# Chunked attention and a snake MLP on one core: first V load in two parts, second-layer matmuls dealt out later, one square moved from GpSimd to ScalarE

## Chip, cores and metric

The kernel runs on one NeuronCore of a Trainium2 chip. The metric is the device time of one execution in microseconds (us), given as the median of several runs. Engines are TensorE (PE: matmuls; PEld: its weight loads), VectorE (DVE), ScalarE (ACT), GpSimd (POOL) and SyncE (SP).

## The reference, cut to what matters

There are 4 batches, 8 heads, 768 positions and a head size of 64. Each chunk of 32 queries attends to 8 memory keys and to a window of keys from 16 before the chunk to 8 after it. The result, 3072 tokens of 512, goes through an MLP of width 2048.

```python
for c in range(S // 32):
    l_start, r_end = max(0, 32 * c - 16), min(S, 32 * c + 32 + 8)
    k_full = concat([mem_k, k[:, :, l_start:r_end]]); v_full = concat([mem_v, v[:, :, l_start:r_end]])
    out[:, :, 32 * c:32 * c + 32] = softmax(q_c @ k_full.T / 8) @ v_full
x = out.transpose(0, 2, 1, 3).reshape(3072, 512)
h = x @ w_in
g = h + sin(alpha * h) ** 2 / (alpha + 1e-9)
result = g @ w_out
```

## The kernel before

The batches are worked through one after the other, and each engine runs its instructions in the order in which the program issues them.

**Attention.** The queries of a head are cut into 8 blocks of 96 (`QW`, `NJ`). For one cell (a pair of heads and a block) the scores are one matmul per head, whose 128 rows are the keys of that block with the memory keys among them (`qk`, L265 to L275). A unit is four cells. `exps` (L277) takes the exponentials on ScalarE, three to four instructions a unit, masked by the bias. `pv` (L294) multiplies them with V, 65 columns a head, of which the last gives the sum, and VectorE divides (L305, L306). `xt` (L313) transposes the block on TensorE and copies it to `xT` (L325). V stands in `vws`, one buffer for even and one for odd batches; `load_v` (L126) fills heads times blocks `n0` to `n1` with four DMAs on GpSimd's queue (L139): two large ones and two for the rows that neighbouring blocks share.

**The first burst.** `first_burst` (L348) does batch 0's attention in an order written out by hand in `ORDER` (L14): `k`, `q` turn a pair of heads of K and Q by transposes, `s` are a unit's scores, `e` its exponentials, `v` its product with V, `x` its transposes and copy, and `z` warming matmuls on zeros (`spin`, L157; each 128x512). `xt` adds two of these ahead of its transposes for the units whose block has a PSUM tile of its own (units 2 to 7, L316). After `e 7` a sine of one column is taken, which brings in ScalarE's table for sines (L375). The copies of units 4, 5 and 6 are ScalarE's, the others VectorE's.

**Loads at the start.** GpSimd's queue issues, in this order: K and Q of batch 0 in pairs of heads with V's first 16 (heads 0 and 1) among them, V 16 to 32, V 32 to 64 (heads 4 to 7), four quarters of w_in (`load_w_in`, L201), K and Q of batch 1 (`load_qk`, L117), two halves of w_out (`load_w_out`, L207).

**The first MLP layer.** `l1` does one of 16 groups (ft) of 128 features for the 768 tokens of a batch: eight matmuls of 384 columns into one PSUM tile `hT` of two banks (L400), or for ft 3, 7 and 11 of batch 0 into two tiles `hs` of the small pool (`split`); a sine on ScalarE (L412, or L409 in halves); and a square, which a string of letters gives to DVE, ACT or POOL (L518 to L520; L421, L415, L417). `finish` then combines on VectorE: `gT = s / alpha + hT` (L429, or L425 in halves). `finish` of a group is called in the loop's next step, ahead of that step's `l1`. In batch 0 the one of ft 11 is held back (`late`, L529) until that of ft 12 is issued. The pool `big` (PSUM) has three buffers of two banks for scores, products and `hT`, the pool `smp` two of one bank for the second layer's `o`, for transposes and for `hs`.

**The second MLP layer.** `l2` (L440) is a generator of 96 matmuls a batch, 16 for each of 6 blocks of 128 tokens, 128x512 each (L449, L479; for batch 0 the first two blocks go in halves, so that they end at matmuls 24 and 32). A finished block is copied (`put_out`, L437; even blocks VectorE, odd ones ScalarE) and stored by SyncE. The class `Stream` (L24) deals these matmuls out: `take(n)` adds n to a debt and issues matmuls until it is paid; without `through`, it also returns at the end of a block and keeps the rest of the debt for the next call.

**The order of the main loop** (L499). For each batch: 16 steps of the first layer, with `take(2)` in each from ft 1 on (`take(3)` in the last batch) of the batch before; then this batch's second layer joins the stream; then, in batch 0 alone, K and Q of batch 1 are turned in eight pieces with 4 + 8 x 3 matmuls between; in batches 1 and 2 those of the next batch were turned within the 16 steps. Then `burst` (L330) does the next batch's attention in steps of one block, with the step's entry of `shares` dealt in three parts between scores, product and transposes (the product lags by 3 steps in the first such burst and by 1 in the others), and then `take(3)`. The last batch's 96 matmuls run alone at the end.

Of the kernel before, what the change touches and what calls it, by code (L numbers as in the profile page):

```python
# [12 lines left out]
KW = 856  # L13
ORDER = (  # L14
    "k 0,q 0,memk 0,memv 0,k 1,s 0,e 0,z 1,s 1,e 1,q 1,k 2,s 2,e 2,s 3,v 0,q 2,e 3,k 3,x 0,v 1,q 3,s 4,e 4,x 1,"
    "s 5,e 5,z 1,v 2,s 6,e 6,z 2,v 3,x 2,v 4,s 7,e 7,x 3,v 5,x 4,v 6,x 5,v 7,x 6,x 7"
)
BF = mybir.dt.bfloat16
F32 = mybir.dt.float32
ACTF = mybir.ActivationFunctionType  # L20
# [29 lines left out]
def kernel(  # L50
# [12 lines left out]
    nc = tc.nc  # L63
# [25 lines left out]
    rows = consts.tile([P, 6], F32, name="rows")  # L89
# [36 lines left out]
    def load_v(b, n0, n1):  # L126


        vw = vws[b % 2].rearrange("p h j c -> p (h j) c")
        vf = v[b].rearrange("h s d -> (h s) d")  # L130
        vf = vf.rearrange("(n p) d -> p n d", p=QW)
        parts = (
            (vw[16:64, n0:n1, 0:D], vf[0:48, n0:n1]),
            (vw[72:120, n0:n1, 0:D], vf[48:96, n0:n1]),
            (vw[0:16, n0 + 1:n1, 0:D], vf[80:96, n0:n1 - 1]),
            (vw[120:128, n0:n1 - 1, 0:D], vf[0:8, n0 + 1:n1]),
        )
        for dst, src in parts:
            nc.gpsimd.dma_start(dst, src)  # L139
# [14 lines left out]
    zeros = consts.tile([P, 512], BF, name="zeros")  # L154
    nc.vector.memset(zeros[:], 0.0)  # L155

    def spin(n, z=None):  # L157

        if z is None:
            z = smp.tile([P, 512], F32, name="z", tag="sm")  # L160
        for _ in range(n):
            nc.tensor.matmul(z[:], zeros[:, 0:P], zeros[:])  # L162
# [26 lines left out]
        out=biasm[:], in0=rows[:, 0:5], scalar1=1.0, scalar2=-NEG, op0=ALU.subtract, op1=ALU.mult)  # L189
    nc.scalar.copy(memk_bf[:], memk_f[:])  # L190
    load_v(0, 16, 32)
    load_v(0, 32, 64)
    with nc.allow_non_contiguous_dma(reason="alpha transpose load"):
        nc.sync.dma_start(alpha_sb[:], moe_alpha.rearrange("(ft p) -> p ft", p=P))

# [81 lines left out]
    def exps(cells, sc):  # L277
        pt = pts[state["n"] % NPT]
        state["n"] += 1
        for m in range(3):  # L280
            cols = [((1 if j == 0 else 0), 4, (2 if j == NJ - 1 else 3))[m] for _, j in cells]
            c0 = 0
            for c1 in range(1, 5):
                if c1 < 4 and cols[c1] == cols[c0]:
                    continue
                nc.scalar.activation(  # L286
                    pt[:, 0:H * QW].rearrange("p (g e c) -> p e g c", g=4, e=2)[:, :, c0:c1, 32 * m:32 * m + 32],
                    sc[:, :, 0:4 * QW].rearrange("p g (e c) -> p g e c", e=4)[:, :, c0:c1, 32 * m:32 * m + 32],
                    ACTF.Exp, bias=biasm[:, cols[c0]:cols[c0] + 1], scale=0.125,
                )  # L290
                c0 = c1
        return pt
# [17 lines left out]
        )  # L310
        return x_blk, ot

    def xt(dst, x_blk, ot, copy=nc.vector.tensor_copy):  # L313
        if ot is None:
            z = smp.tile([P, 512], F32, name="z", tag="sm")
            spin(2, z)  # L316
            xtp = z[:].bitcast(BF)[:, 0:KT * QW]
        else:
            xtp = ot[:].bitcast(BF)[:, 0, 640:640 + KT * QW]
        xtp = xtp.rearrange("p (k c) -> p k c", k=KT)  # L320
        for kt in range(KT):
            nc.tensor.transpose(  # L322
                xtp[:, kt, :], x_blk[:, 2 * kt:2 * kt + 2, :].rearrange("p e d -> p (e d)"), ident[0:QW, 0:QW]
            )
        copy(dst, xtp)  # L325
# [4 lines left out]
    def burst(b, stream, shares, lag):  # L330

        xT = xp.tile([P, KT, S], BF, name="xT")
        ptl, xbl = {}, {}
        for s in range(NJ + lag + 1):
            n = shares[s] if s < len(shares) else 0
            if s < NJ:
                ptl[s] = exps(row(s), qk(row(s)))
            stream.take(n // 3, True)
            if 0 <= s - lag < NJ:
                xbl[s - lag] = pv(b, row(s - lag), ptl.pop(s - lag))  # L340
            stream.take((n + 1) // 3, True)
            if 0 <= s - lag - 1 < NJ:
                j = s - lag - 1
                xt(xT[:, :, QW * j:QW * j + QW], *xbl.pop(j))
            stream.take((n + 2) // 3, True)
        return xT

    def first_burst(kq):  # L348

        xT = xp.tile([P, KT, S], BF, name="xT")  # L350
        cells = [[(u // 2, 4 * (u % 2) + c) for c in range(4)] for u in range(8)]
        scl, ptl, xbl = {}, {}, {}
        for what, n in [t.split() for t in ORDER.split(",")]:
            n = int(n)
            if what == "k":
                t_k(kq[0], n)
            elif what == "q":
                t_q(kq[1], n, nc.vector.tensor_copy if n == 1 else nc.scalar.copy)
            elif what == "memk":
                mt = smp.tile([P, HP, 32], BF, name="mt", tag="sm")  # L360
                for hp in range(HP):
                    nc.tensor.transpose(
                        mt[:, hp, :],
                        memk_bf[0:32, 2 * hp:2 * hp + 2, :].rearrange("p e d -> p (e d)"),
                        ident[0:32, 0:32])
                nc.vector.tensor_copy(memkT[:], mt[:])
                put_memk(0)
            elif what == "memv":
                put_memv(0)
            elif what == "s":  # L370
                scl[n] = qk(cells[n])
            elif what == "e":
                ptl[n] = exps(cells[n], scl.pop(n))
                if n == 7:
                    nc.scalar.activation(rows[:, 0:1], zeros[:, 0:1], ACTF.Sin)  # L375
            elif what == "z":
                spin(n)
            elif what == "v":
                x_blk, ot = pv(0, cells[n], ptl.pop(n))
                xbl[n] = x_blk, (ot if n < 2 else None)  # L380
            elif what == "x":
                hf = n % 2
                xt(xT[:, n // 2, HALF * hf:HALF * hf + HALF].rearrange("p (k c) -> p k c", k=KT),
                   *xbl.pop(n), nc.scalar.copy if n in (4, 5, 6) else nc.vector.tensor_copy)
        return xT


# [106 lines left out]
    stream = Stream()  # L494
    xT = first_burst(kq)
# [3 lines left out]
    for i in range(B):  # L499
        gT = gp.tile([P, FT, S], BF, name="gT")  # L500
        last = i == B - 1
        at_ft = {2 * n: n for n in range(8)}
        pieces = []
        if not last:
            srcs = [(kq_next[n % 2], n // 2) for n in range(2 * HP)]
        state["pools"] = 1

        def pair_to(n):
            while len(pieces) < min(n, 2 * HP):
                pieces.append(pair_up(*srcs[len(pieces)], nc.vector.tensor_copy if i == 0 and len(pieces) in (2, 4, 6) else None))  # L510

        def piece(n):
            pair_to(n + 3)
            (t_k if n % 2 == 0 else t_q)(pieces[n], n // 2)

        if 0 < i < B - 1:
            pair_to(2)
        finish, late = None, None  # L518
        for ft in range(FT):
            sq = ("DADPADAPADAPDAAA" if i == 0 else "ADAAPDADADAPADAD")[ft]  # L520
            if 1 <= ft:
                stream.take(3 if last else 2)
            if 0 < i < B - 1 and ft in at_ft:
                piece(at_ft[ft])
            if i == 0 and ft == 8:
                pair_to(2)
            if i == 0 and ft == 13:
                load_v(1, 0, H * NJ)
            if finish is not None and ft - 1 == 11 and i == 0:  # L529
                late = finish  # L530
            elif finish is not None:
                finish()
                if late is not None:
                    late()
                    late = None
            finish = l1(i, ft, xT, gT, sq, i == 0 and ft in (3, 7, 11))
        finish()
        stream.add(l2(i, gT, last))
        if not last:
            if i == 0:  # L540
                state["pools"] = 0
                stream.take(4)
                for n in range(2 * HP):
                    piece(n)
                    stream.take(3, True)
                put_memv(1)
            if i + 2 < B:
                kq_next = load_qk(i + 2)
            if i == 0:
                xT = burst(i + 1, stream, (5, 5, 5, 4, 4, 4, 4, 4, 3, 3, 3, 3), 3)  # L550
            else:
                xT = burst(i + 1, stream, (16, 8, 6, 6, 6, 5, 5, 5, 5, 5), 1)
            if i + 2 < B:
                put_memk(i + 2)
            stream.take(3)
            if i + 2 < B:
                load_v(i + 2, 0, H * NJ)
                put_memv(i + 2)
# [31 lines left out]
```

The softmax here doesn't subtract the row's maximum and nothing guards it: scores larger than these inputs give would overflow.

## Time and profile before

| What | Value |
|---|---|
| median of 7 runs | 233.82 us (233.18 to 234.45) |
| profiled execution | 233.18 us |
| its span in the profile | 231.4 us |
| busy: PE, DVE, ACT, POOL | 219.4, 160.1, 152.3, 70.0 us |
| first layer's matmuls of batch 0 begin | 26.90 us |
| second layer's matmuls of the last batch end | 228.2 us |
| HBM read, written | 28.94 MB, 6.29 MB |

The span is the time between the first and last instruction of the profiled execution; all times of day in this document count from its start. A line of a view names the engine, the source line (L400 is line 400 of the kernel) and, as "out<-in", the tiles. Matmuls overlap, so one that is listed with 0.326 us (128x384) follows the one before it by less. An idle time in brackets is that of the engine just before the instruction, with what ended it.

### The profile page before, as it was taken

How to read it: one execution, taken by the hardware profiler on the slowest of the kernel's cores; microseconds unless marked ns; L12 is line 12 of the kernel's file. 1: busy time of each engine (PE TensorE's matmuls, PEld its weight loads, DVE VectorE, ACT ScalarE, POOL GpSimd, SP SyncE). 2: the span in 40 equal slices, each digit the busy share in tenths (PEclk: the TensorE clock that was granted, in tenths of full speed). 3: DMA queues.
4: the chain of work that ended last, by engine and by line, in shares of the span. 5: the costliest groups of instructions: out<-in, count | busy, mean ns of one | idle time of the engine just before them, and what ended most of it. 6: DMA issues, size and time to landing. Idle time of an engine off the chain costs nothing.

```text
span 231.4 us, 4595 instructions
## 1 busy us (share of the span) xinstructions
PE 219.4 (95%) x1842; PEld 122.7 (53%) x1842; DVE 160.1 (69%) x288; ACT 152.3 (66%) x246; POOL 70.0 (30%) x80
## 2 busy tenths in 40 slices
PE   7998899989999999999999999998999999899994
PEld 3455555555446556554555656664555555454453
DVE  5776588988568897987566789887565468784110
ACT  2578689793987387888664877978665676880110
POOL 8998122585812115167200314020000020100000
PEclk9999999999999999999999999999999999999999
DMA  6999999999999900119992101010111010101112
GB/s 85 151 174 177 204 204 206 208 145 88 175 223 158 92 30 0 48 8 191 164 151 73 45 0 48 0 45 3 45 48 70 24 47 0 45 0 48 73 64 91
DMA packets 51805, 21.13 MB, mean 91 GB/s; under 512 B 36296, under 2 KB 48840, under 8 KB 51784
## 3 DMA queue, kind: packets, MB, share of 16 engines
q0 software_dynamic: 45568, 14.41, 72.2%
q1 hardware_dynamic: 6216, 6.43, 9.3%
q8 instruction: 14, 0.23, 0.4%
q14 instruction: 7, 0.06, 0.1%
HBM read 28.94 MB, written 6.29 MB: 152 GB/s over the span
## 4 chain that ended last, share of the span: by engine, by line
PE 62%; ACT 12%; DVE 9%; POOL 7%; issue 5%; DMA 2%; POOLq 1%; DVEq 0%; ACTq 0%
PE o L479 28%; PE hT L400 21%; DVE gT L429 5%; ACT u L412 4%; POOL vw L139 3%; PE ot L301 3%; ACT pt L286 3%; PE sc L270 2%; DMA vw<-in_v_dram 2%; DVE s L421 2%; ACT s L415 2%; PE tt_a L242 2%; PE ot L322 2%; PE o L468 2%; PE o L449 1%
## 5 line engine op out<-in xcount | busy, mean ns | idle before, releaser
L479 PE MATMUL o<-w_out_sb,gT 128*128 128x512 bf16 x336 | 90.0, 380 | 0.4 <-DVE gT L429 0.4
L400 PE MATMUL hT<-xT,w_in_sb 128*128 128x384 bf16 x488 | 87.1, 326 | 2.9 <-DVE gT L429 2.8
L429 DVE SCALAR_TENSOR_TENSOR gT<-s,inv_alpha,hT 128x768 bf16<-128x768 f32 x61 | 61.0, 1012 | 19.7 <-ACT s L415 11.2
L412 ACT ACTIVATE u<-hT,alpha_sb 128x768 f32<-128x768 f32 x61 | 54.7, 897 | 24.5 <-PE hT L400 23.5
L400 PEld LDWEIGHTS <-w_in_sb 128*128 128x128 bf16 x512 | 49.3, 98 | 37.5 <-issue 3.8
L286 ACT ACTIVATE pt<-sc,biasm 128x256 bf16<-128x256 f32 (+2 forms) x104 | 39.1, 470 | 15.2 <-PE sc L270 15.2
L479 PEld LDWEIGHTS <-gT 128*128 128x128 bf16 x336 | 29.3, 98 | 24.3 <-DVE gT L429 1.2
L417 POOL TENSOR_TENSOR s<-u 128x768 f32<-128x768 f32 x9 | 13.2, 1465 | 87.5 <-ACT u L412 61.3
L415 ACT ACTIVATE s<-u 128x768 f32<-128x768 f32 x32 | 27.0, 843 | 1.0
L421 DVE TENSOR_TENSOR s<-u 128x768 f32<-128x768 f32 x23 | 24.3, 1056 | 2.3 <-ACT u L412 2.2
L306 DVE TENSOR_TENSOR x_blk<-ot,rinv 96x512 bf16<-96x512 f32 x32 | 22.0, 686 | 1.1
L139 POOL DMA_DIRECT2D vw<-in_v_dram x24 | 21.9, 925 | 0.2 <-issue 0.2
L216 POOL COPY pr<-q_bf 128x768 bf16<-128x768 bf16 x12 | 10.7, 895 | 35.5 <-PE tt_a L242 24.4
L437 DVE COPY o_sb<-o 128x512 f32<-128x512 f32 x12 | 8.3, 690 | 15.6 <-PE o L479 15.4
L437 ACT COPY o_sb<-o 128x512 f32<-128x512 f32 x11 | 6.4, 583 | 17.9 <-PE o L479 17.9
L305 DVE RECIPROCAL rinv<-ot 96x8 f32<-96x8 f32 x32 | 6.4, 201 | 15.7 <-PE ot L301 15.5
L301 PEld LDWEIGHTS <-pt 128*128 128x128 bf16 x256 | 11.7, 98 | 6.8 <-issue 2.5
L162 PE MATMUL z<-zeros 128*128 128x512 bf16 x40 | 12.8, 427 | 1.9 <-DVE zeros L155 1.2
L301 PE MATMUL ot<-vw,pt 128*128 128x65 bf16 x256 | 13.0, 193 | 1.0 <-DMA vw<-in_v_dram 0.4
L242 PEld LDWEIGHTS <-pr 128*128 128x128 bf16 x144 | 10.0, 98 | 5.9 <-DVE pr L216 0.9
L270 PEld LDWEIGHTS <-kTi 64*128 64x128 bf16 x256 | 6.8, 94 | 11.4 <-PE ot L322 5.5
L322 PEld LDWEIGHTS <-x_blk 96*128 96x128 bf16 x128 | 8.7, 97 | 7.3 <-DVE x_blk L306 1.5
(76 smaller groups left out, 170.0 us busy)
## 6 DMA issues: line engine op xcount, KB each, us to landing
out_dram<-o_sb SPq DMA_DIRECT2D x23, 256.0 KB, 2.5
k_bf<-in_k_dram POOLq DMA_DIRECT2D x3, 768.0 KB, 7.7
q_bf<-in_q_dram POOLq DMA_DIRECT2D x3, 768.0 KB, 12.6
vw<-in_v_dram POOLq DMA_DIRECT2D x6, 384.0 KB, 14.9
w_in_sb<-in_moe_w_in_dram POOLq DMA_DIRECT2D x4, 512.0 KB, 9.7
w_out_sb<-in_moe_w_out_dram POOLq DMA_DIRECT2D x2, 1024.0 KB, 24.2
k_bf<-in_k_dram POOLq DMA_DIRECT2D x4, 192.0 KB, 5.1
q_bf<-in_q_dram POOLq DMA_DIRECT2D x4, 192.0 KB, 5.2
```

The source lines that it names most:

```text
L139: nc.gpsimd.dma_start(dst, src)
L242: nc.tensor.transpose(t[:, r, :], src[:, r].rearrange("p e d -> p (e d)"), ident[:])
L286: nc.scalar.activation(pt[:, 0:H * QW].rearrange("p (g e c) -> p e g c", g=4, e=2)[:, :, c0:c1, 32 * m:32 * m + 32], sc[:, :, 0:4 * QW].re ...
L301: nc.tensor.matmul(otv[:, n // 4, n % 4, :], pt[:, QW * n:QW * n + P], vws[b % 2][:, 2 * hp + n % 2, j, 0:D + 1])
L306: nc.vector.tensor_tensor(out=x_blk[:].rearrange("p (g e) d -> p g e d", g=2), in0=otv[0:QW, :, :, 0:D], in1=rv.unsqueeze(3).to_broadcast( ...
L400: nc.tensor.matmul(hts[hf][:, 0:HALF], w_in_sb[:, kt, P * ft:P * ft + P], xT[:, kt, HALF * hf:HALF * hf + HALF], start=(kt == 0), stop=(kt ...
L412: nc.scalar.activation(u[:], hT[:, :, 0:HALF], ACTF.Sin, scale=alpha_sb[:, ft:ft + 1])
L415: nc.scalar.activation(s2[:], u[:], ACTF.Square)
L421: nc.vector.tensor_tensor(out=s2[:], in0=u[:], in1=u[:], op=ALU.mult)
L429: nc.vector.scalar_tensor_tensor(out=gv, in0=s2[:], scalar=inv_alpha[:, ft:ft + 1], in1=hT[:, :, 0:HALF], op0=ALU.mult, op1=ALU.add)
L437: (nc.vector.tensor_copy if s % 2 == 0 else nc.scalar.copy)(o_sb[:], o[:])
L479: nc.tensor.matmul(o[:], gT[:, ft, P * s:P * s + P], w_out_sb[:, ft, :], start=(ft == 0), stop=(ft == FT - 1),)
```

## The change

- Batch 0's V for heads 4 to 7 is loaded in two calls, heads 4 and 5, then 6 and 7: eight DMAs in place of four.
- In `ORDER`, `v 4` goes behind `s 7` and `e 7`.
- The warming matmuls ahead of the transposes of units 2 to 7 were two each; they become 2, 2, 1, 1, 0, 0.
- The sine of one column after `e 7` goes.
- Unit 3's copy to `xT` goes from VectorE to ScalarE.
- The square of ft 11 of batch 0 goes from GpSimd to ScalarE, and its `finish` is not held back any more.
- The shares of the bursts are smaller: 41 in place of 47 in the first, 63 in place of 67 in each of the other two, so that more of a batch's 96 matmuls is left for the next batch's 16 steps.

```diff
@@ ORDER
-    "s 5,e 5,z 1,v 2,s 6,e 6,z 2,v 3,x 2,v 4,s 7,e 7,x 3,v 5,x 4,v 6,x 5,v 7,x 6,x 7"
+    "s 5,e 5,z 1,v 2,s 6,e 6,z 2,v 3,x 2,s 7,e 7,v 4,x 3,v 5,x 4,v 6,x 5,v 7,x 6,x 7"
@@ loads
-    load_v(0, 32, 64)
+    load_v(0, 32, 48)
+    load_v(0, 48, 64)
@@ xt
-    def xt(dst, x_blk, ot, copy=nc.vector.tensor_copy):
+    def xt(dst, x_blk, ot, copy=nc.vector.tensor_copy, warm=0):
...
-            spin(2, z)
+            spin(warm, z)
@@ first_burst
-                if n == 7:
-                    nc.scalar.activation(rows[:, 0:1], zeros[:, 0:1], ACTF.Sin)
...
-                   *xbl.pop(n), nc.scalar.copy if n in (4, 5, 6) else nc.vector.tensor_copy)
+                   *xbl.pop(n), nc.scalar.copy if n in (3, 4, 5, 6) else nc.vector.tensor_copy,
+                   (0, 0, 2, 2, 1, 1, 0, 0)[n])
@@ main loop
-            sq = ("DADPADAPADAPDAAA" if i == 0 else "ADAAPDADADAPADAD")[ft]
+            sq = ("DADPADAPADAADAAA" if i == 0 else "ADAAPDADADAPADAD")[ft]
...
-            if finish is not None and ft - 1 == 11 and i == 0:
+            if finish is not None and False:
                 late = finish
...
-                xT = burst(i + 1, stream, (5, 5, 5, 4, 4, 4, 4, 4, 3, 3, 3, 3), 3)
+                xT = burst(i + 1, stream, (5, 5, 4, 4, 4, 3, 3, 3, 3, 3, 2, 2), 3)
             else:
-                xT = burst(i + 1, stream, (16, 8, 6, 6, 6, 5, 5, 5, 5, 5), 1)
+                xT = burst(i + 1, stream, (16, 8, 6, 5, 5, 5, 5, 5, 4, 4), 1)
```

## The prediction

> **What bounds the kernel now.** I read the page's shares first, then the chain of waits around the first MLP pass, then the timeline of each engine in the tails of the four passes. "Pass i" is the first MLP layer of batch i (16 groups ft), "burst i" the attention of batch i, "outputs" are the second layer's matmuls, which the stream deals out between other work; M, u, s, g stand for a group's matmuls, sine, square and its VectorE combination. The page's part 1:
>
> ```profile
> PE 219.4 (95%) x1842; PEld 122.7 (53%) x1842; DVE 160.1 (69%) x288; ACT 152.3 (66%) x246; POOL 70.0 (30%) x80
> ```
>
> TensorE is busy 95% of the span. So only two things pay: fewer matmuls on its path, or its last 12.0 us of gaps (231.4 - 219.4) made smaller. The chain of waits from 20 to 30 us shows where the first pass comes from (start, length, what):
>
> ```profile
> 16.36 5.20 DMA vw<-in_v_dram
> ...
> 21.69 0.40 PE ot L301 x8
> 22.09 0.30 PE sc L270 x8
> ...
> 22.41 1.35 ACT pt L286 x4
> ...
> 23.78 1.28 ACT L375
> ...
> 25.07 0.20 ACT rows L375
> 25.27 0.38 ACT xT L325
> ...
> 25.69 0.59 PE z L162 x2
> 26.29 0.17 PE z L322 x4
> ...
> 27.06 3.09 PE hT L400 x19
> ```
>
> The V load of heads 4 to 7 holds unit 4; the last scores (s 7) queue behind it; the last exponentials, the dummy sine with its table load, and the copy of block 4 follow; only then is a PSUM buffer free for block 6. By the timeline pass 0 starts at 26.90. In the tails of the passes TensorE waits for VectorE, which combines the groups; its timeline at the end of pass 0, of pass 2 and of pass 3 (start, length, engine, line, operation, in brackets the idle time and who ended it):
>
> ```profile
> 48.00 1.46 PE L400 MATMUL hT<-xT,w_in_sb 128*128 128x384 bf16 x8 [0.58 <-DVE gT L429]
> ...
> 157.21 0.35 PE L270 MATMUL sc<-qT,kTi 64*128 64x96 bf16 x8 [0.58 <-DVE gT L429]
> ...
> 201.07 2.76 PE L400 MATMUL hT<-xT,w_in_sb 128*128 128x384 bf16 x16 [0.88 <-DVE gT L429]
> ...
> 210.52 14.20 PE L479 MATMUL o<-w_out_sb,gT 128*128 128x512 bf16 x65 [0.38 <-DVE gT L429]
> ```
>
> Elsewhere a pass steps by 1.30 for eight matmuls (0.163 each) and 0.43 for two outputs (0.216 each), without gaps.
>
> **What the Trainium skill says.** "ScalarE: Activation LUTs", What ACT_TABLE_LOAD costs: a load takes 1283 ns plus about 1380 ns of drain, an activation with immediate operands 186 ns + 0.833 ns per element. The trace agrees on the load (1.28) and the square (0.64 + 0.19 = 0.83; measured 0.843), not on the drain: the next instruction starts 0.01 after the load. "DMA: Bandwidth & Descriptors", Anatomy of one DMA: 2.0 us + bytes/436e3, so 2.45 for 192 KB. The first K load took 4.3 from issue to landing; I use that. "GPSIMD Engine Reference", Specifications: it shares SBUF interfaces with VectorE. The trace agrees: VectorE's square of ft 12 takes 1.38 at 45.45, beside GpSimd's square of ft 11 (44.55 to 46.02), against 0.95 alone. "TensorE: Matmul & The Clock Gate", What's actually happening: a clock that falls after an idle window of some 3.4 us. The page's PEclk is 9 everywhere, also at 46 to 48 us where TensorE is busy 1.42 of 2.00 us.
>
> **Part 1: the first burst.** Unit 4 goes behind s 7, six warming matmuls go (blocks 4 and 5 one each, 6 and 7 two each: 6 x 0.216 = 1.30), the dummy sine goes, block 3's copy moves to ScalarE. Block 2's transposes end at 21.26. s 7 needs no late V and its buffer (unit 2's) is free at 20.37, so it runs at 21.26, its exponentials from 21.65 to 23.0 (now 22.41 to 23.76: 0.76 earlier). Unit 4 follows at 21.54. The V load: GpSimd issued four 16-head parts in 2.65 (4.88 to 7.53), so heads 4 and 5 are issued from 13.89 to 16.55; parts landed 4.2 to 5.3 after issue in the load before, so the last, issued near 15.9, lands at 20.1 to 21.2: in time. Heads 6 and 7 are issued until 19.2 and land by 22.8 to 23.9; unit 6 wants them at 23.1, and TensorE's cover ends at 23.9, when VectorE is through with unit 5. From there VectorE is the bound: per unit 0.20 + 0.69 (0.92 with gaps), unit 4's product from 22.24 to 22.93, unit 7's ends at 22.93 + 3 x 0.92 = 25.7, transposes 0.2, **pass 0 starts at 26.0, 0.9 earlier**. Block 3's copy on ScalarE (0.42) runs right behind the exponentials, at 23.0; behind it on that queue wait blocks 4 to 6, which aren't ready sooner. On VectorE it frees 0.36. The dummy sine (1.28 + 0.20) leaves the path: the load now stands before u of ft 0, and ScalarE is idle there from block 6's copy (25.4) to M's end (27.3); it costs 0 as long as that gap exceeds 1.28, as at 73.69, where the load ran ahead of a wait of 3.78; else up to 0.9.
> The four more V issues push GpSimd's queue back 19.2 - 17.04 = 2.15: w_in's four parts, batch 1's K and Q, w_out. The first w_in quarter now lands at 17.04 + 6.9 = 23.94, 2.4 after V's last byte; later it lands 2.4 after 22.8 to 23.9: 25.2 to 26.3, needed at 26.0. Bounds: start 0.9 earlier, or 0.2 if it is late by 0.7. Later quarters (26.4, 29.2, 31.8 now, each some 1.5 later) are needed at 31, 36 and 42; w_out's (44.4, 47.6) at 49 and 54: hidden.
>
> **Part 2: ft 11 of pass 0.** The square leaves GpSimd (1.47) for ScalarE (0.84), and its combination (two of 0.57) is no longer held back behind ft 12's. ScalarE was idle 0.93 ahead of u of ft 13, so that isn't delayed. Behind the new square wait u of ft 12 (0.85 later) and on VectorE: g of ft 11 (1.1) now stands before s and g of ft 12. With everything 0.9 earlier, g of ft 10 ends at 44.6, g 11 at 45.7, s 12 at 46.65 (0.95, since GpSimd is quiet), g 12 at 47.7 (now 47.95). M of ft 15 waits for just that buffer (first line of the last fence): 0.25 to 0.3 earlier, and with it u, s and g of ft 15 and the pair copy at 52.37. So of the 0.9, **0.3 reaches the end of the pass**; 0.6 goes to the new order. Bounds: none (start at 26.7: +0.4) to all 0.9. Batch 1's V issue, 4.30 at 45.96, moves up some 4.5; it is behind w_out's bytes anyway and its last part, landed near 60, is wanted at 63.8: 0.
>
> **Part 3: shifted outputs.** I counted the stream's deals by the loop's rules. Batch 0's burst gives up 6 outputs to pass 1 (24 left, not 18): 2 each at ft 10, 11, 12. The later bursts give up 4, and the three after them stop at output 64, which ends a row block: 6 fewer in all (64, not 70). Pass 2 takes 32 (4 at ft 1, two at ft 14 and 15), pass 3 takes 32, to ft 10.
> - Burst 1: until 65.92 ScalarE's exponentials are the bound (four of 1.20 back to back, TensorE idle 0.42), so the output taken from step 2 gives nothing. Steps 5 and 6 give 2 x 0.216 = 0.43. From 71.4 VectorE steps by 1.10 per unit against TensorE's 1.07, so steps 7, 10, 11 give nothing: -0.43.
> - Pass 1's tail: M 10 at 96.16, M 12 at 99.17 and M 14 at 102.87 wait for VectorE. The 0.43 ahead of M 10, 11 and 12 puts M 12 at 100.06, u 12 at 101.45 (now 100.66), u 13 0.85 late, g 12 0.5, g 13 0.55; the next burst's first scores wait for g 13's buffer: **+0.57**. Sum -0.43 + 0.57 = +0.15.
> - Bursts 2 and 3 are TensorE's own (ScalarE waits 0.4 to 1.1 for every step): 6 x 0.216 = -1.30 each. Pass 2 grows by 1.30, of which the gap from 156.46 to 157.21 takes 0.75: +0.55; sum -0.75.
> - Pass 3: 0.65 more ahead of M 9, 1.30 ahead of M 10. u 11 goes from 200.57 to 201.85, GpSimd's square behind it from 201.53 to 202.8, g 11 to g 15 end 0.95 late, and the second layer's 16th matmul (last line above) waits for g 15: +0.95; sum -0.35.
>
> Total -0.30 + 0.15 - 0.75 - 0.35 = **-1.25**. The profiled execution took 233.18 (span 231.4 and 1.8 around it), the lowest of the runs; it becomes 231.9. Against the median of 233.82, 0.64 higher, I forecast **232.6**.
>
> **Rivals.** (a) The tails take the moved outputs whole. For: the TensorE gaps there (0.75 in pass 2, some 1.5 in pass 3) are about what is put in. Against: the gaps are filled ahead of a chain u, s, g that then runs late. Each tail at 0: -0.9 - 0.43 - 1.30 - 1.30 = -3.9: 229.9. (b) The late w_in quarter or V part holds pass 0 to 26.7: part 1 and 2 give +0.4 instead of -0.3: 233.3, no change. For: GpSimd's queue is 2.15 longer. Against: DMA has bytes queued throughout. (c) **Slower**: the six outputs and the ScalarE eviction that ends their row block (0.57) fall whole into the last groups' chain, in all three tails: 1.87 each against bursts of 0.43, 1.30 and 1.30. -0.30 + 1.44 + 2 x 0.57 = +2.3: 236.1. It decides once the three tails grow by more than 3.3 together. For: the eviction that closes a batch moves from ft 9 to ft 12, 15 and 10. Against: ScalarE idles 0.4 to 1.1 at many groups there. (d) The clock falls without the warming matmuls: an estimate from that page is up to 1.7 for one window at half rate; TensorE stays some 70% busy at 22 to 26 us, as it did at full clock elsewhere. I give it almost nothing.
>
> **Chances.** Forecast 0.50 (of it 0.07 lands within the bound), (a) 0.17, (b) 0.18 (0.13 within, 0.03 faster, 0.02 slower), (c) with (d) 0.15 (0.01 within). 0.3% is 0.7 us, about what a measurement here can tell from no change. Faster 0.63, same 0.21, slower 0.16. The likeliest's own range is 231.6 to 233.4. The full one reaches most of (a) and all of (b): 230.3 to 234.4.
>
> **What would show it.** Right: first scores s 7 before unit 4, no wait for vw, no table load between exponentials and copies, M 0 near 26.0; M 15 of pass 0 near 47.7; passes 1 to 3 starting earlier by about 0.7, 1.5 and 2.2. Wrong: an idle time ahead of M 0 ended by w_in, or ahead of unit 6 by vw; pass 3's g 11 not waiting for GpSimd; tails of passes 1 to 3 that grow by nothing, or by more than 1.3.

## The result and the profile after

The changed kernel is slower: 236.48 us as the median of 13 executions (234.55 to 240.16), against 233.88 us for the kernel before (34 executions on the same chip), a ratio of 1.0084 with a 95% interval of 1.0065 to 1.0104. The forecast was 232.6 us, with a range up to 234.4.

The profiled execution, which is not among the 13, took 239.63 us (span 237.8), and its TensorE clock fell for a while. The ratio leaves out such slow executions, those over 238 us, and so it stands below what this trace and the median show. The page's first part, and below it the clock by slices (40 slices, so some 6 us each):

```profile
PE 222.9 (94%) x1836; PEld 123.2 (52%) x1836; DVE 158.6 (67%) x287; ACT 154.2 (65%) x247; POOL 69.7 (29%) x83
...
PEclk9999769999999999999999999999999999999999
```

TensorE has six matmuls fewer and is busy 3.5 us longer: in slices 5 and 6 it was granted less clock (half of it from 27.0 to 33.8 us, 6.83 us long), and its gaps grew from 12.0 to 14.9 us.

The chain of waits from 4 to 35 us (start, length, what) has another cause for the start of pass 0 than before. There it ran over the V load, the last exponentials and the dummy sine; here it runs over GpSimd's queue and w_in:

```profile
4.16 5.95 DMA q_bf<-in_q_dram
...
10.40 5.92 DMA q_bf<-in_q_dram
...
16.61 0.61 POOL vw L139
...
17.35 2.62 POOL vw L139 x4
19.97 8.21 DMA w_in_sb<-in_moe_w_in_dram
...
28.22 6.81 PE hT L400 x24
```

TensorE's timeline at the same places as before (in brackets the idle time and who ended it): the start of pass 0, its M 15, the end of pass 2, and pass 3.

```profile
28.22 6.81 PE L400 MATMUL hT<-xT,w_in_sb 128*128 128x384 bf16 x24 [2.22 <-DMA w_in_sb<-in_moe_w_in_dram]
...
52.69 1.46 PE L400 MATMUL hT<-xT,w_in_sb 128*128 128x384 bf16 x8 [1.20 <-DVE gT L429]
...
163.27 0.34 PE L271 MATMUL sc<-qT,kTi 64*128 64x96 bf16 x8
...
210.54 2.76 PE L400 MATMUL hT<-xT,w_in_sb 128*128 128x384 bf16 x16 [0.87 <-DVE gT L429]
...
216.96 5.35 PE L479 MATMUL o<-w_out_sb,gT 128*128 128x512 bf16 x24 [0.43 <-DVE gT L429]
```

Pass 0 waits 2.22 for w_in; the 24 matmuls that took 4.07 take 6.81, most of it at half clock. The wait of M 15 rose from 0.58 to 1.20. Pass 2's gap of 0.58 ahead of the next scores is filled. Pass 3 still has two waits of the old length, 0.87 and 0.43 (0.88 and 0.38 before), but the longer one now stands ahead of M 14 and not of M 12. And there are waits of a kind that the kernel before had none of. TensorE's waits from 60 us on (total, times, longest):

```profile
PE ot L302 <- DVE xT L326: 0.9, 3, 0.5
PE tt_a L243 <- DVE o_sb L437: 0.6, 1, 0.6
...
PE ot L323 <- DVE x_blk L307: 0.3, 1, 0.3
```

Three products of attention wait for VectorE's copy of a transposed block, and a transpose waits for a copied row block of the output. VectorE's timeline ahead of the first of these waits shows why:

```profile
71.25 0.69 DVE L307 TENSOR_TENSOR x_blk<-ot,rinv 96x512 bf16<-96x512 f32 x1
71.86 0.68 DVE L437 COPY o_sb<-o 128x512 f32<-128x512 f32 x1
72.46 0.34 DVE L326 COPY xT<-ot 128x384 bf16<-128x384 bf16 x1
73.29 0.20 DVE L306 RECIPROCAL rinv<-ot 96x8 f32<-96x8 f32 x1 [0.49 <-PE ot L302]
```

The smaller shares let row block 2 of the second layer end later, so that its copy (0.68) now stands between a product and the block copy that frees the PSUM buffer for the next product. In the kernel before, the same copy stood one step earlier, in a step that waits for ScalarE's exponentials:

```profile
65.54 0.69 DVE L437 COPY o_sb<-o 128x512 f32<-128x512 f32 x1 [0.40 <-PE o L479]
...
65.92 0.41 PE L301 MATMUL ot<-vw,pt 128*128 128x65 bf16 x8 [0.42 <-ACT pt L286]
```

The work from one M 0 to the next scores ("pass") and from there to the next M 0 ("burst") can be set against the kernel before. The columns are differences in us; the third is from the kernel e8 below, in which those copies are moved.

| Stage | predicted | changed kernel | e8 |
|---|---|---|---|
| burst 1 | -0.43 | +0.42 | -0.18 |
| pass 1 | +0.57 | +0.63 | +0.63 |
| burst 2 | -1.30 | -1.06 | -1.46 |
| pass 2 | +0.55 | +1.43 | +1.03 |
| burst 3 | -1.30 | -0.91 | -1.32 |
| pass 3 and the end | +0.95 | +1.28 | +1.30 |
| sum | -0.96 | +1.79 | 0.00 |

Pass 0 and the start are left out. (The clock had long recovered by burst 1, and e3 below, where it never fell, has the same +0.42: M 0 of pass 0 to M 0 of pass 1 is 50.78 against 50.36.)

### The profile page after: what moved, and what is told of

It reads as the page before. It is cut to its first block, busy times and chain, and to the rows that moved or that the text cites. A ratio compares the mean times of both kernels' runs of the same rounds, so it can differ in the third digit from the quotient of the medians.

```text
span 237.8 us, 4592 instructions
## 1 busy us (share of the span) xinstructions
PE 222.9 (94%) x1836; PEld 123.2 (52%) x1836; DVE 158.6 (67%) x287; ACT 154.2 (65%) x247; POOL 69.7 (29%) x83
## 4 chain that ended last, share of the span: by engine, by line
PE 56%; DVE 14%; ACT 10%; DMA 8%; issue 7%; POOL 4%; POOLq 1%; DVEq 0%; ACTq 0%
PE o L479 23%; PE hT L400 21%; DMA q_bf<-in_q_dram 5%; DVE gT L429 5%; DMA w_in_sb<-in_moe_w_in_dram 3%; DVE s L421 3%; ACT u L412 3%; PE ot L302 2%; DVE x_blk L307 2%; ACT s L415 2%; ACT pt L287 2%; PE sc L271 2%; PE tt_a L243 2%; PE o L468 1%; PE o L449 1%
## 5 line engine op out<-in xcount | busy, mean ns | idle before, releaser
L400 PE MATMUL hT<-xT,w_in_sb 128*128 128x384 bf16 x488 | 90.3, 333 | 5.0 <-DVE gT L429 2.7
L479 PE MATMUL o<-w_out_sb,gT 128*128 128x512 bf16 x336 | 91.1, 380 | 0.4 <-DVE gT L429 0.4
L400 PEld LDWEIGHTS <-w_in_sb 128*128 128x128 bf16 x512 | 50.2, 100 | 41.7 <-issue 7.0
L479 PEld LDWEIGHTS <-gT 128*128 128x128 bf16 x336 | 29.9, 98 | 24.8 <-DVE gT L429 1.4
L417 POOL TENSOR_TENSOR s<-u 128x768 f32<-128x768 f32 x8 | 11.7, 1465 | 87.5 <-ACT u L412 67.2
L415 ACT ACTIVATE s<-u 128x768 f32<-128x768 f32 x33 | 27.8, 843 | 1.0
L421 DVE TENSOR_TENSOR s<-u 128x768 f32<-128x768 f32 x23 | 23.4, 1016 | 5.7 <-ACT u L412 5.6
L139 POOL DMA_DIRECT2D vw<-in_v_dram x28 | 24.0, 868 | 1.0 <-DMA q_bf<-in_q_dram 0.8
L162 PE MATMUL z<-zeros 128*128 128x512 bf16 x34 | 11.8, 455 | 1.2 <-DVE zeros L155 1.2
```

Of the source, the lines that this page charges most:

```text
L400: nc.tensor.matmul(hts[hf][:, 0:HALF], w_in_sb[:, kt, P * ft:P * ft + P], xT[:, kt, HALF * hf:HALF * hf + HALF], start=(kt == 0), stop=(kt ...
L415: nc.scalar.activation(s2[:], u[:], ACTF.Square)
L421: nc.vector.tensor_tensor(out=s2[:], in0=u[:], in1=u[:], op=ALU.mult)
L479: nc.tensor.matmul(o[:], gT[:, ft, P * s:P * s + P], w_out_sb[:, ft, :], start=(ft == 0), stop=(ft == FT - 1),)
```

## The experiments

The theory after this reading: the change is a gain in the first burst, a loss by ft 11, a loss by the shares (because of where the copies of row blocks fall), and a V load in two calls that makes w_in late. The rival is the prediction's own accounting, with the shares a gain. Each part was first run alone.

**e1: the V load in two calls alone.**

```diff
-    load_v(0, 32, 64)
+    load_v(0, 32, 48)
+    load_v(0, 48, 64)
```

> The kernel before with one edit: V for heads 4 to 7 of batch 0 in two calls. Theory A (the four more DMAs are what costs: the first w_in quarter comes late): it lands near 28 in place of 23.9, pass 0 begins near 28.2 in place of 26.9, so about +1.3 (235.2), and in some runs TensorE's clock falls as well, up to +4.5 (238). Rival, the prediction's own step: it lands by 26.3, ahead of the 26.9 at which it is needed, so 233.9, no change.

Measured: 233.54 against 233.75, ratio 1.0007 (0.9986 to 1.0029). The executions fall into two groups: 15 of 22 lie between 233.0 and 234.1, the others between 234.6 and 236.4. The profiled one belongs to the second (235.31). TensorE's timeline there:

```profile
28.63 4.07 PE L401 MATMUL hT<-xT,w_in_sb 128*128 128x384 bf16 x24 [1.49 <-DMA w_in_sb<-in_moe_w_in_dram]
```

So w_in can be late already without the other edits; the two groups suggest that it is so in some executions and not in others. Here the clock did not fall in an idle time of 1.49; in two of the seven slower executions the granted clock was lower, 0.990 and 0.993.

**e2: the whole change, V in one call.**

```diff
-    load_v(0, 32, 48)
-    load_v(0, 48, 64)
+    load_v(0, 32, 64)
```

> The changed kernel with V for heads 4 to 7 in one call again. Theory A: no wait for w_in, pass 0 begins near 26.0, the clock stays, and the runs no longer scatter over 5 us; about 2 below the changed kernel's undisturbed runs: 233.7. By the prediction's sum without its late-w_in case: 232.6. If the V load is not the cause, it stays at 235.8 with scatter.

Measured: 235.25 (235.06 to 235.48), ratio 1.0066 (1.0052 to 1.0081). Pass 0 starts at 26.70 without a wait for w_in, the clock is full, and the scatter is gone, but the expected 233.7 did not come. The two calls cost 236.48 - 235.25 = 1.2 at the median of all executions; by the ratios (1.0084 and 1.0066) they cost 0.4, within the intervals. The other 1.5 has other causes.

**e3: the smaller shares alone.**

```diff
-                xT = burst(i + 1, stream, (5, 5, 5, 4, 4, 4, 4, 4, 3, 3, 3, 3), 3)
+                xT = burst(i + 1, stream, (5, 5, 4, 4, 4, 3, 3, 3, 3, 3, 2, 2), 3)
...
-                xT = burst(i + 1, stream, (16, 8, 6, 6, 6, 5, 5, 5, 5, 5), 1)
+                xT = burst(i + 1, stream, (16, 8, 6, 5, 5, 5, 5, 5, 4, 4), 1)
```

> The kernel before with one edit: the smaller shares of the three bursts. Theory B (the moved output matmuls cost by themselves): stage by stage as in the changed kernel's profile, burst 1 +0.4, pass 1 +0.6, burst 2 -1.1, pass 2 +1.4, burst 3 -0.9, pass 3 +1.3: +1.8, 235.7. Rival, the prediction's part 3: -0.95, 232.9.

Measured: 235.80 against 233.75, +2.05, ratio 1.0083 (1.0068 to 1.0099). By the stages of its trace it is +1.82 with the start of pass 0 left out. The prediction's -0.95 did not come. TensorE's waits from 60 us on are those of the changed kernel:

```profile
PE ot L301 <- DVE xT L325: 0.9, 3, 0.5
PE tt_a L242 <- DVE o_sb L437: 0.6, 1, 0.6
```

**e4: ft 11 alone** (its square on ScalarE, its `finish` not held back).

```diff
-            sq = ("DADPADAPADAPDAAA" if i == 0 else "ADAAPDADADAPADAD")[ft]
+            sq = ("DADPADAPADAADAAA" if i == 0 else "ADAAPDADADAPADAD")[ft]
...
-            if finish is not None and ft - 1 == 11 and i == 0:
+            if finish is not None and False:
```

> The kernel before with one edit: the square of ft 11 of batch 0 on ScalarE and its combination not held back. The prediction's part 2: g of ft 11 ahead of ft 12's holds the last group's buffer, +0.6 at the end of pass 0: 234.5. Rival: VectorE's shorter square of ft 12 (0.95 for 1.38) and GpSimd's free time pay for it: 233.9 or less.

Measured: 234.48 against 233.75, +0.73, ratio 1.0035 (1.0020 to 1.0050). The timeline of TensorE shows the place, M 15 of pass 0, which waited 0.58 before:

```profile
49.49 1.46 PE L400 MATMUL hT<-xT,w_in_sb 128*128 128x384 bf16 x8 [1.20 <-DVE gT L429]
```

This is what the prediction had: g of ft 11 stands ahead of s and g of ft 12, and M 15 needs that buffer.

**e5: the first burst alone**, V in one call.

```diff
-    "s 5,e 5,z 1,v 2,s 6,e 6,z 2,v 3,x 2,v 4,s 7,e 7,x 3,v 5,x 4,v 6,x 5,v 7,x 6,x 7"
+    "s 5,e 5,z 1,v 2,s 6,e 6,z 2,v 3,x 2,s 7,e 7,v 4,x 3,v 5,x 4,v 6,x 5,v 7,x 6,x 7"
...
-            spin(2, z)
+            spin(warm, z)
...
-                if n == 7:
-                    nc.scalar.activation(rows[:, 0:1], zeros[:, 0:1], ACTF.Sin)
...
-                   *xbl.pop(n), nc.scalar.copy if n in (4, 5, 6) else nc.vector.tensor_copy)
+                   *xbl.pop(n), nc.scalar.copy if n in (3, 4, 5, 6) else nc.vector.tensor_copy,
+                   (0, 0, 2, 2, 1, 1, 0, 0)[n])
```

> The kernel before with only the edits of the first burst (unit 4 behind s 7, warming matmuls 2, 2, 1, 1, 0, 0, no sine of one column, block 3's copy on ScalarE); V is loaded as before, in one call. The prediction gives pass 0 a start 0.9 us earlier; with ft 11 as before, all of it should come through to the end: 233.75 - 0.9 = 232.9. The difference of the runs so far (the change without the V split is +1.5, smaller shares alone +2.05, the square alone +0.7) gives 1.5 - 2.05 - 0.7 = -1.2: 232.5. A rival says that the gain is lost before it reaches the end, because pass 0's tail stands on GpSimd's square of ft 11 and on the later loads: 233.75. A clock that falls without the warming matmuls would show in the granted clock and give 235 or more.

Measured: 232.67 against 233.83, -1.16, ratio 0.9955 (0.9940 to 0.9969). TensorE's timeline: s 7 ahead of unit 4, which still waits for V, no warming matmuls at the end, and VectorE as the last releaser:

```profile
21.60 0.34 PE L270 MATMUL sc<-qT,kTi 64*128 64x96 bf16 x8
22.38 0.40 PE L301 MATMUL ot<-vw,pt 128*128 128x65 bf16 x8 [0.43 <-DMA vw<-in_v_dram]
...
26.32 0.34 PE L322 MATMUL z<-ident,x_blk 96*128 96x96 bf16 x4 [0.49 <-DVE x_blk L306]
26.50 3.74 PE L399 MATMUL hT<-xT,w_in_sb 128*128 128x384 bf16 x22
```

The clock stays full (0.998 to 1.0 in all executions): with w_in in time, the warming matmuls are not needed to keep it. From pass 0 on, each stage is as long as in the kernel before, within 0.01, so that all of an earlier start comes through. One trace can't give the size of that start: 26.50 is 0.40 ahead of the 26.90 before, but e3, e4, e6, e7 and e9, whose first burst is that of the kernel before, start pass 0 at 27.09 to 27.77. The medians give the -1.16.

The parts add up: -1.16 + 0.73 + 2.05 = +1.62 against +1.50 measured for e2.

**e6 and e7: the shares of the first burst alone, and of the later two alone.** Each is one half of e3's diff.

> The kernel before with only the first burst's shares made smaller (41 in place of 47). The prediction has burst 1 -0.43 and pass 1 +0.57, +0.15 in sum: 233.9. The reading of the changed trace has burst 1 +0.42, since there the loop from a product over its sum, division and copy to the next product sets the step of 1.69 and an eviction of 0.68 stands in it, and pass 1 +0.55: +1.0, 234.7.

> The kernel before with only the later two bursts' shares made smaller (63 in place of 67). The prediction has -0.75 for burst 2 with pass 2 and -0.35 for burst 3 with pass 3: -1.1, 232.65. The stages of the kernel with both shares give -0.43 (or -1.06, read from the changed kernel) and +0.53, so +0.1 to -0.5 for the first pair if the stages don't depend on what went before, and +0.4 for the second: 233.7 to 234.3. If the two are not independent of the first burst's shares, the sum of this run and of the one with the first burst's shares alone is not the +2.05 measured for both.

Measured: e6 234.97 against 233.83, ratio 1.0056 (1.0040 to 1.0073); e7 234.82, ratio 1.0048 (1.0029 to 1.0067). By the stages e6 is +1.03 (0.41 in burst 1, 0.62 in pass 1 with what follows it up to the next M 0) and e7 +0.77, together 1.80 against e3's 1.82. The two are independent. e7 was above what was expected (233.7 to 234.3); the four figures of the changed kernel's column in the table (-1.06, +1.43, -0.91, +1.28) add up to +0.74, which is what came.

**e8: all smaller shares, four copies moved to ScalarE.** Beside e3's diff:

```diff
-        (nc.vector.tensor_copy if s % 2 == 0 else nc.scalar.copy)(o_sb[:], o[:])
+        on_act = s % 2 or (i < 3 and s == 2) or (i == 1 and s == 4)
+        (nc.scalar.copy if on_act else nc.vector.tensor_copy)(o_sb[:], o[:])
```

> The kernel before with all the smaller shares, and with the copies of row block 2 of batches 0 to 2 and of row block 4 of batch 1 moved from VectorE to ScalarE. If what the smaller shares cost is these copies, which the later deals place in the middle of VectorE's chain (waits of 0.46, 0.24, 0.24 and 0.64 us of TensorE behind them), 1.2 to 1.6 of the 2.05 come back: 234.2 to 234.6. If the moved matmuls themselves cost it (tails that take the outputs whole, bursts that are set by their loop and not by TensorE), the copies make no difference: 235.8. If ScalarE's own chain suffers from four copies of 0.58, it gets worse: over 236.

Measured: 233.75 against 233.83, ratio 1.0000 (0.9988 to 1.0013). The whole 2.05 came back, more than expected. TensorE's waits from 60 us on no longer have a copy of VectorE's ahead of a product:

```profile
PE hT L400 <- DVE gT L429: 1.2, 2, 0.9
PE sc L270 <- DVE gT L429: 0.5, 1, 0.5
PE o L480 <- DVE gT L429: 0.4, 1, 0.4
PE ot L301 <- ACT pt L286: 0.4, 1, 0.4
PE ot L322 <- DVE x_blk L306: 0.3, 1, 0.3
PE tt_a L242 <- ACT o_sb L438: 0.2, 1, 0.2
```

**e9: the four copies alone**, with the shares of before.

> The kernel before, its shares too, with only the four copies (row block 2 of batches 0 to 2, row block 4 of batch 1) moved from VectorE to ScalarE. If the copies cost only where the smaller shares put them, they stand in gaps here and nothing changes: 233.8, within 0.3. If VectorE's chain pays for them in any place, this kernel gains by itself, 0.5 to 2.0, and the smaller shares cost as much with the copies moved as without: 231.8 to 233.3. A loss, over 234.2, would mean that ScalarE's chain takes them worse than VectorE's.

Measured: 233.72 against 233.82, ratio 0.9991 (0.9980 to 1.0002). By the stages, with the start left out, it is 0.30 shorter than the kernel before (0.15 in burst 2, 0.15 in burst 3). So the four copies cost 0.3 on VectorE where the old shares put them, and 1.8 (e3 against e8, by the stages) where the smaller ones do. With e8 this shows the cause: it is not the copy, and not the moved matmuls, but the two together. It shows also that with the copies out of the way the smaller shares gain nothing.

**e10: the whole change, V's heads 4 to 7 in six DMAs instead of eight** (`which` picks from the four parts).

```diff
-    load_v(0, 32, 48)
-    load_v(0, 48, 64)
+    load_v(0, 32, 48, (0, 1))
+    load_v(0, 32, 64, (2, 3))
+    load_v(0, 48, 64, (0, 1))
```

> The changed kernel with six DMAs for V's heads 4 to 7 in place of eight: the two large parts in two calls, the two small ones in one. If the lateness of w_in comes from the time that GpSimd takes for each issue (0.67 a DMA), the first w_in quarter is issued 1.35 earlier, near 18.6, the wait of TensorE ahead of pass 0 falls from 2.2 in the disturbed execution to under 1, and the clock falls in few executions or none: a median of 235.3 to 235.8 and no execution over 237. If it comes from the order of the bytes, nothing changes: 236.5, up to 240.

Measured: 234.75 (234.36 to 235.97), ratio 1.0048 (1.0031 to 1.0065), below the 235.3 to 235.8 that was expected. At the medians it is 1.7 below the changed kernel, by the ratios 0.8. GpSimd's timeline has w_in 1.67 earlier than in the changed kernel (19.97), and TensorE's no wait ahead of pass 0:

```profile
16.04 2.27 POOL L139 DMA_DIRECT2D vw<-in_v_dram  x3 [0.30 <-DMA q_bf<-in_q_dram]
18.30 3.00 POOL L204 DMA_DIRECT2D w_in_sb<-in_moe_w_in_dram  x4
```

```profile
25.70 4.07 PE L401 MATMUL hT<-xT,w_in_sb 128*128 128x384 bf16 x24
```

What made w_in late is thus the issues ahead of it on GpSimd's queue. The clock is at 0.998 or more in all 13 executions, without any warming matmuls added. Whether the split, once it is cheap enough, is a gain by itself is not shown: e10 is 0.4 below e2 by the ratios, within the intervals.

**e11: the whole change with eight warming matmuls right ahead of pass 0.**

```diff
                    (0, 0, 2, 2, 1, 1, 0, 0)[n])
+        spin(8)
         return xT
```

> The changed kernel with eight warming matmuls (1.73 us) right ahead of pass 0. If the executions over 237 come from a clock that falls in the idle time ahead of pass 0, they go: the granted clock is 1.0 throughout, pass 0 starts at 27.7 to 28.3, and all executions lie between 236.0 and 237.5, median 236.6. If they come from a w_in that lands later still, they remain, up to 240, and the others get slower by up to 1.7.

Measured: ratio 1.0132 (1.0104 to 1.0160); 237.11 as the median of five executions, 236.14 to 237.70, all with a granted clock of 0.998 or more. The sixth, of which the trace is, and one of the kernel before took over 780 us and are left out, so no trace shows the place. None of the five goes to 240, and they are slower than the changed kernel's executions at full clock by some 1.7, about what eight such matmuls take. In the changed kernel seven of 13 executions had a clock of 0.998 or more and took 234.55 to 236.48; the six others had 0.986 to 0.993 and took 237.25 to 240.16. So the tail above 237 goes with a lower clock, and the one trace of such an execution has the fall in TensorE's wait for w_in. e2, e10 and e11, which take that wait away or fill it with warming matmuls, have no execution with a lower clock among their 24.

**e12: the gains together**: e5's edits and e10's load.

> The kernel before with the edits of the first burst and with V's heads 4 to 7 in six DMAs (the two large parts in two calls, the two small ones in one). In the kernel with the first burst's edits alone unit 4's product still waits 0.43 for the V load in one call, and the bound moved from there to VectorE; the changed kernel with six DMAs was 0.5 below the one with one call. So 0.4 to 0.8 less than the 232.67 of the first burst's edits: 231.9 to 232.3. If the later issue of w_in (1.3) eats it: 232.7 or more, with executions over 234 where TensorE waits for w_in.

Measured: 232.49 against 233.69, ratio 0.9947 (0.9929 to 0.9964). It beats both kernels, as e5 does, but its 0.2 under e5 lies within the intervals; the expected 0.4 to 0.8 did not come. Five of its eight executions took 232.0 to 232.6, the other three 233.0 to 233.7. The profiled one is the slowest of the three (233.65), and its trace shows neither of the two loads in question as the cause: unit 4 does not wait for V, and w_in lands at 26.59, ahead of pass 0 at 27.06. The burst is late from its start, where TensorE waits 0.54, 0.36 and 0.59 for K and Q of batch 0 (the longest such wait in e5 is 0.41), and pass 0 up to the next scores is 0.28 longer than in e5. What holds the other two stays open.

## Why the prediction was wrong

**Part 1, right for TensorE, wrong in one load.** s 7 ran first (at 21.41 in the changed kernel), unit 6 did not wait for V, the table load (1.28 at 25.70) cost nothing, and TensorE's last transposes ended at 26.0, the time forecast. e5 gives -1.16 for the forecast -0.9. The step of part 1 that failed is w_in: "it lands 2.4 after 22.8 to 23.9: 25.2 to 26.3, needed at 26.0", with a bound of 0.7 for its lateness. V's last part landed at 23.24, inside the forecast, but w_in came 4.9 after it and not 2.4: it was issued at 19.97, not 19.2, for the queue stood 0.83 on an earlier load, and it landed 8.21 later, at 28.2. The prediction took the gap of 2.4 from the kernel before, where the DMA engines had bytes queued all the time. Its sentence "DMA has bytes queued throughout" was false for the change. The stretches from 18 to 22 us (last column GB/s), of the kernel before and then of the changed one, show the queue running dry while GpSimd issues small parts:

```profile
18.00:20.00 2.00, 1.89 (x31) 1.14 (x32) 0.88 (x3) 2.00 (x7) 2.00 (x3) 1.00 2.27 153
20.00:22.00 2.00, 1.54 (x24) 0.93 (x21) 1.52 (x4) 1.44 (x5) 1.39 (x3) 1.00 1.26 187
```

```profile
18.00:20.00 2.00, 1.71 (x30) 1.10 (x31) 0.77 (x4) 2.00 (x7) 2.00 (x5) 1.00 1.22 75
20.00:22.00 2.00, 1.97 (x33) 1.23 (x32) 1.65 (x4) 1.87 (x7) 2.00 (x3) 1.00 1.30 84
```

The rate falls to 75 and 84 GB/s. By the packets of the two traces, there are never fewer than 16 in flight at once in these 4 us in the kernel before; in the changed one there are fewer than 12 for a third of the time, and at one moment only 2.

Rival (b) named this place with the wrong size (0.7, not 2.2), and rival (d), "almost nothing", came true in 6 of 13 executions: not for want of warming matmuls alone, as e5 and e10 show, but because the late w_in leaves TensorE idle. Whether the warming matmuls that went make such falls more frequent is open: e1, which keeps them and has w_in late in some executions, has a lower clock in only two of 22. In the profiled execution pass 0 itself is 3.37 longer up to its last M, where e2's is 0.63 longer: 2.7 by the clock.

**Part 2, right.** The forecast 0.6 was +0.73 in e4's time, 0.57 in its trace.

**Part 3, wrong in sign.** -0.95 was forecast; e3 gives +2.05. This miss of 3.0 is what decided.
- The main failure is a step that is missing. The deals were counted, and with them where each row block ends (row block 2 of batch 0 later in the burst, for one), but the copy that each end brings was priced only in rival (c), and there on ScalarE and in the tails. Row block 2 in the bursts and row block 4 in pass 2 fall to VectorE, and the prediction put their copies at nothing. The table puts 0.60 of it into burst 1 (+0.42 against -0.18), 0.40 each into burst 2 and pass 2, and 0.41 into burst 3 (-0.91 against -1.32): 1.8. e8 and e9 show it.
- "Burst 1: steps 5 and 6 give 2 x 0.216" failed on its own too: with the copies moved, the burst gives 0.18. While scores are still in the rotation, products are 1.68 apart in the kernel before, in e3 and in e8 alike, whatever TensorE has to fill the time. The step is set by an exchange of VectorE and TensorE: the product's result (0.4), the reciprocal of its sum and the division (0.20 + 0.69), the copy of the block before (0.34), which frees the buffer of the next product. In the changed kernel VectorE's reciprocals of these steps stand at 73.29, 74.97 and 76.66, and each ends an idle time of 0.49; those of the kernel before, at 68.05, 69.73 and 71.41, do the same. That TensorE was busy there before is because outputs filled the loop. What e8 does gain in this burst comes after these steps, where the fifth and sixth product are 1.07 apart and not 1.28.
- Bursts 2 and 3, "TensorE's own", were right: -1.46 and -1.32 in e8 for the forecast -1.30 (of which e9 gives 0.15 each to the copies).
- Pass 1 was right (+0.63 for +0.57). Pass 2's +0.55 has the right mechanism (the gap ahead of the next scores is filled) but lacks a delay at ft 8, where a transpose waits for the copy of row block 4: the step from M 7 to M 8 takes 2.87 in e3 and 2.46 in e8, against 2.07 before. With 0.8 and 0.4 more the forecast would have been 1.35 and 0.95, for the measured 1.43 and 1.03.
- Pass 3: the chain was right, its size not: +1.30, not +0.95. The prediction put GpSimd's square 1.27 later and let g 11 to g 15 end only 0.95 later. Counted from M 0, M 11 comes 1.25 later in e3, and g 11 and g 15 both come 1.30 later, with a wait of 0.87 (ahead of M 14) and one of 0.43 left behind them. This tail grows by all of the six moved outputs (1.30), as rival (c) held.
- Rival (c)'s 236.1 is near the measured time, and the three tails grow by 0.63, 1.43 and 1.28, together 3.34, just over the 3.3 from which it was to decide. But its mechanism, outputs and a ScalarE eviction that fall whole into each tail (1.87 each), is not what happened: the tail of pass 1 took a third of it, 0.40 of the tail of pass 2 goes when a VectorE copy is moved, and the bursts, which (c) priced as the forecast did, came out 1.5 worse. That its total fits is luck.

In sum, by the runs at full clock: -1.16 (first burst), +0.73 (ft 11), +2.05 (shares) make +1.6 where the prediction had -1.25; V in two calls adds 0.4 by the ratios, 1.2 at the median of all executions, and up to 5 in single ones.

## What to carry to other kernels

Work dealt out as filler has consequences of its own: when its place is changed, follow the copy and the buffer that its end brings, engine by engine, because a copy of 0.68 us that costs next to nothing in one step costs 0.4 to 0.6 in the next. An engine that looks busy may only be filling another loop; taking filler away pays only if the loop doesn't set the step. And a load that is split to come earlier takes an issue slot for every part from all loads behind it: share the small parts, and look at what is needed next.

## What the runs showed of the hardware that was not expected

- GpSimd stood still ahead of a load's issue until the one eight issues earlier had landed: 0.54 at 10.40 us (the 12th load, until the 4th was there) and 0.83 at 16.61 (the 20th, until the 12th) in the changed kernel, and 0.91 at 16.83 (the 19th, until the 11th) in e12. In the traces these loads use eight semaphores in turn, and the load that stands waits for the one that it shares with that earlier load, so this is the program's doing and not the chip's.
- The TensorE clock went to half within 1.0 us of the start of an idle time (26.0 to 27.0) and stayed there for 6.83 us, 5.6 of them with TensorE at work again. In the 3.41 us before the fall TensorE had been busy for 1.68. An idle time of 1.49 in e1 left the clock alone, though TensorE was busy for only 1.37 of the 3.41 us up to its end; and in e8's profiled execution, whose first burst is that of the kernel before with all its warming matmuls, the clock was at half for 3.41 us from 19.48 on, where the longest idle time nearby was 0.82 and TensorE had been busy for 1.92 of the 3.41 us before. The Trainium skill's "TensorE: Matmul & The Clock Gate", What's actually happening, on which the prediction's rival (d) rested, ties a fall to an idle window of some 3.4 us. Ahead of these two falls TensorE wasn't idle from end to end of any such stretch; the measurement decides. What does set off a fall is not shown: neither the length of one idle time nor the busy share just before it tells these cases apart.
- With V's small parts shared (six DMAs for eight) the same bytes came early enough; the executions' spread fell from 5.6 us to 1.6.
